# A state-space scan followed by a bilinear feed-forward layer: a new program order, with B and C taken in float32 by head

## The chip, the cores and the metric

The kernel runs on one core of a Trainium2 chip. The core has five engines that work side by side and meet through semaphores: PE multiplies matrices (PEld is its loading of weights), DVE and ACT work on vectors and evacuate PE's results from PSUM, POOL works on vectors in SBUF, and SP issues transfers, which 16 DMA engines carry out. The metric is device time in microseconds from the start to the end of one execution.

## The reference

The inputs are x (4 batches, 8 heads, 768 positions, 32 wide), a (one decay a position), B and C (16 wide), and the matrices w1, w2 (256 x 1024), w3 (1024 x 1024) and w_out (1024 x 256).

```python
for c in range(nc):                               # chunks of positions
    cum = np.cumsum(la, axis=-1)                  # la = log(clip(a))
    M = np.einsum('bhin,bhjn->bhij', Cc, Bc) * np.exp(cum_i - cum_j) * causal
    y = einsum(M, xc) + einsum(Cc, state) * exp(cum)
    state = exp(sum(la)) * state + sum_j(Bc_j * xc_j * exp(cum_last - cum_j))
x = y.transpose(0, 2, 1, 3).reshape(B * S, H * D) # 3072 tokens of 256
out = (((x @ w1) * (x @ w2)) @ w3) @ w_out
```

The matrices arrive as 64-bit floats, so every weight has to be turned into float32 on the chip, out of its two 32-bit words.

## The kernel before

**Slabs and chunks.** The 768 positions are cut into 8 slabs of 96, each slab into two chunks of T = 48 (so 16 chunks, c0 to c15; the chunk length is free, since the state is carried exactly). A slab of all four batches has 384 tokens.

**A chunk** (`chunk`, line 286) makes the decays with two bf16 matmuls (`decay`, 298, tile `pd`) and an exponential on ACT (`expo`, 304, into R); POOL scales B (`bw`, 309); `cb` (314) multiplies C by B into `pc`; DVE weights it with the decays (`weigh`, 328); `Mx` (333) multiplies by x into `py`. XE holds x with two heads in one block-diagonal 128 x 64 operand, so 16 products do a chunk's 32 heads and batches. `Z` (346) transposes the state out of `py` and DVE copies it into the next chunk's XE in four small copies; `hi` and `lo` (361, 365) leave the output as two float32r parts in xT.

**B and C.** For the first slab `cb` uses float32 operands laid out by `load_first`. For the others each is loaded raw, split into three bf16 parts on ACT, DVE and POOL (`split_slab`, 225), written to DRAM, read back packed six times 16 rows high (`load_pack`, 249), and multiplied in bf16 with 96 rows.

**The layer.** `up` (487) makes one column tile of 128 of x @ w1 and of x @ w2 for a slab, each as six float32r products of high and low parts. `gate_a` (506, ACT) evacuates the first, `gate_b` (510, DVE) multiplies by the second, `gate_hi` (513, ACT) and `gate_lo` (518, POOL) make the two parts, and `down` (523) multiplies by w3 @ w_out, which the chip makes once: 16 steps `v*.M` (454) of 4 float32 products each, accumulated in four PSUM banks, then split by `e*.a` and `e*.b`.

**Weights.** `from_f64` (384) does one item of 512 KB: load (D), scaling (A), a byte copy (Y), shift and mask (L), shift and or (S); items of w1 and w2 have two more steps, H and P, for the two parts. There are 8 items `w*`, 4 items `o*` (w_out) and 16 items `v*` (w3). ON_VECTOR (46) and ON_POOL (49) say where some steps run.

**Order.** For the first two slabs PLAN (21) is an order written out by hand: each name is a step, issued in that order on its engine, and "+24" is 24 matmuls of zeros (`keep_clock`, 578). From line 590 on the scheduler is free to order everything but PE, and the loop at line 607 does one slab after another: `up`, then `down`, with the next slab's two chunks between the `up` tiles. All loads and stores are issued by SP. PSUM has four banks for the scan and four for the layer.

Of the kernel before, what the change touches and what calls it, by code (L numbers as in the profile page):

```python
# [45 lines left out]
ON_VECTOR = """
o0.A o1.Y o2.Y o3.A v0.A v0.Y v11.A v14.A v3.Y v5.A v7.Y v8.Y w0.H w1.Y w2.A w3.H w3.Y w4.A w5.H w6.A w6.H
""".split()
ON_POOL = "s1.rB s1.rC s2.rB".split()

@with_exitstack
def kernel(
# [31 lines left out]
    N, D = Bn.shape[2] * 2 // (CPS * NB * H), x.shape[3] // (NB * H)  # L84
    TE = T + N
    HP = H // 2
    TOK = NB * SL
# [6 lines left out]
    NGF = 11  # L94

    const = ctx.enter_context(tc.tile_pool(name="const", bufs=1))
    work = ctx.enter_context(tc.tile_pool(name="work", bufs=2))
    dram = ctx.enter_context(tc.tile_pool(name="dram", bufs=1, space=bass.MemoryType.DRAM))
    ps_at = ctx.enter_context(tc.tile_pool(name="ps_at", bufs=4, space=bass.MemoryType.PSUM))
    ps_l = ctx.enter_context(tc.tile_pool(name="ps_l", bufs=1, space=bass.MemoryType.PSUM))  # L100
# [10 lines left out]
    def load(*args):  # L111
        return ins(nc.sync.dma_start(*args))

    def acopy(*args):
        return ins(nc.scalar.copy(*args))  # L115

    def vtt(*args):
        return ins(nc.vector.tensor_tensor(*args))  # L118

    def vcopy(*args):  # L120
        return ins(nc.vector.tensor_copy(*args))  # L121

    def ptt(*args):
        return ins(nc.gpsimd.tensor_tensor(*args))  # L124
# [3 lines left out]


    GF = const.tile([P, NGF, TOK], F32, name="gf")  # L130
    gf_turn = [0]

    def next_gf():
        gf_turn[0] += 1
        return GF[:, (gf_turn[0] - 1) % NGF]

    G8 = NB * HP // 2
    NK = 2 * CPS * 2
    first = GF.rearrange("p a s -> p (a s)")
    C0 = first[:, :NK * G8 * T].rearrange("p (k g t) -> p k g t", k=NK, g=G8)  # L140
    B0 = first[:, NK * G8 * T:NK * (G8 * T + TE)].rearrange("p (k m) -> p k m", k=NK)
    zero = const.tile([P, 512], BF16, name="zero")
    nc.vector.memset(zero, 0.0)
    BN = [const.tile([P, CPS, NB * HP, N], F32, name=f"bn{i}") for i in range(2)]

    NG = NB * HP
    RI, RJ = T, T + 6
    KD = RJ + 3 * NG  # L150
    LD = const.tile([KD, 2, TE], BF16, name="ld")
    RD = const.tile([KD, NG, T], BF16, name="rd")
# [3 lines left out]
    XE = [const.tile([P, NB * HP, 2 * D], F32, name=f"xe{i}") for i in range(2)]  # L156

    NSLOT = 6
    KS = NSLOT * N
    BP = const.tile([KS, NB * HP, CPS, 2, TE], BF16, name="bp")  # L160
    CP = const.tile([KS, NB * HP, CPS, 2, T], BF16, name="cp")


    Q, SQ = P // (NB * H), a.shape[1]
    arkc = work.tile([P, 3, SQ], F32, name="arkc", tag="g", bufs=FT + 1)
    ar, keep, cum = [arkc[:, i] for i in range(3)]
    ct = GF[:, NGF - 1].bitcast(BF16)[:, :3 * SQ].rearrange("p (t s) -> p t s", t=3)
# [4 lines left out]
    def task(name):  # L172
        def put(f):
            tasks[name] = f
            return f
        return put

    @task("k.p")
    def _():
# [7 lines left out]
        for h2 in range(2):  # L187
# [8 lines left out]

    task("k.C")(lambda: ins(nc.gpsimd.memset(C0, 0.0)))
    task("k.X0")(lambda: ins(nc.gpsimd.memset(XE[0], 0.0)))
    task("k.X1")(lambda: ins(nc.gpsimd.memset(XE[1], 0.0)))
    task("k.L")(lambda: vcopy(LD, ldc))  # L200
    task("k.R")(lambda: vtt(RD, rdc.unsqueeze(1).broadcast_to([KD, NG, T]), rdg.unsqueeze(2).broadcast_to([KD, NG, T]),
                            ALU.add))
    task("a")(lambda: load(ar, a))
    task("a.clip")(lambda: ins(nc.vector.tensor_scalar(ar, ar, 1e-6, 1.0, ALU.max, ALU.min)))
    task("a.ln")(lambda: ins(nc.scalar.activation(ar, ar, AF.Ln)))
    task("a.scan")(lambda: ins(nc.vector.tensor_tensor_scan(cum, keep, ar, 0.0, ALU.mult, ALU.add)))
    task("a.t0")(lambda: vcopy(ct[:, 0], cum))
    task("a.r0")(lambda: vtt(cum, cum, ct[:, 0], ALU.subtract))
    task("a.t1")(lambda: vcopy(ct[:, 1], cum))
    task("a.r1")(lambda: vtt(ct[:, 2], cum, ct[:, 1], ALU.subtract))  # L210
    task("a.save")(lambda: load(cd.rearrange("q h g t s -> (q h g) (t s)"), ct.rearrange("p t s -> p (t s)")))


    NQ = P // N
    XW = [t.shape[2] // NQ for t in (Bt, Ct)]
    dparts = [[dram.tile([3, N, NQ * XW[w]], BF16, name=f"d{'bc'[w]}{k}") for k in range(NSL)] for w in range(2)]

    RUNS = ((0, 3, 0, 0), (3, 2, 0, 1), (5, 1, 0, 2))  # L220

    def load_slab(sl):
        load(BN[sl % 2].rearrange("p c g n -> p (c g n)"), Bn[sl])

    def split_slab(sl, w):
        p, k = f"s{sl}.", "BC"[w]
        v = {}

        def part(t):
            return v["o"][:, (t, 2 - t)[w]]  # L230

        def raw():
            v["r"] = work.tile([P, 512], F32, name="raw")[:, :XW[w]]
            v["o"] = work.tile([P, 3, 512], BF16, name="part")[:, :, :XW[w]]
            load(v["r"], (Bt, Ct)[w][sl].rearrange("n (q x) -> (n q) x", q=NQ))

        def rest():
            (ptt if p + "r" + k in ON_POOL else vtt)(v["r"], v["r"], part(0), ALU.subtract)

        return [  # L240
            (p + "R" + k, raw),
            (p + "a" + k, lambda: acopy(part(0), v["r"])),
            (p + "r" + k, rest),
            (p + "b" + k, lambda: acopy(part(1), v["r"])),
            (p + "c" + k, lambda: ptt(part(2), v["r"], part(1), ALU.subtract)),
            (p + "W" + k, lambda: load(dparts[w][sl].rearrange("t n (q x) -> (n q) t x", q=NQ), v["o"])),
        ]

    def load_pack(sl, w):
        dst, src = (BP, CP)[w], dparts[w][sl]  # L250
        for s, n, *t0 in RUNS:
# [3 lines left out]
    def load_x(c):  # L255
        xe = XE[c % 2]
        for h2 in range(2):
            load(xe[64 * h2 + N:64 * h2 + TE].rearrange("p g d -> p (g d)"), x[c, h2])
# [447 lines left out]
```

## Time and profile before

| what | us |
|---|---|
| median of 3 runs (lowest, highest) | 325.01 (323.97, 327.65) |
| the profiled execution | 325.25 |
| its span, first to last instruction | 323.5 |
| PE, DVE, ACT, POOL busy in it | 297.9, 156.1, 147.9, 117.5 |
| first `up` product | 40.87 |
| first `down` product | 107.13 |
| first product of slab 2 | 141.37 |
| last product | 319.52 |

The profile is one execution. In its page, a row of a group reads: line, engine, operation, output<-inputs, shapes, count | busy, mean ns of one | idle time before them and what ended it. A timeline row reads: start, duration, engine, line, operation, and in brackets the idle time just before and its releaser. Nearly all of PE's instructions carry line 109, that of the helper `mm`, so they are told apart by their tiles. Transfers by kind, in issues and size:

```profile
## 3 DMA queue, kind: packets, MB, share of 16 engines
q1 hardware_dynamic: 26224, 44.89, 54.3%
...
st<-in_w3t_dram SPq DMA_DIRECT2D x16, 512.0 KB
xe<-in_x_dram SPq DMA_DIRECT2D x32, 192.0 KB
st<-in_w_dram SPq DMA_DIRECT2D x8, 512.0 KB
db<-part SPq DMA_DIRECT2D x7, 384.0 KB
bp<-db SPq DMA_DIRECT2D x7, 384.0 KB
```

### The profile page before, as it was taken

To read this page: it belongs to the slowest core of one execution; us is meant where nothing else is said; L and a number is where in the kernel's file an instruction comes from. 1 tells how busy PE (TensorE), PEld (TensorE's weight loads), DVE (VectorE), ACT (ScalarE), POOL (GpSimd) and SP (SyncE) were. 2 spreads that over 40 slices of the span, in tenths; PEclk is the share of its full clock that TensorE was granted. 3 is DMA by queue.
4 is the path that set the end of the run, shared out by engine and by line. 5 is a ranking of instruction groups with operands and counts; after the bars stand their busy time and mean duration, and the time that the engine had idled before them with its cause. 6 is when DMAs were issued, how large, how long until landed. Compare 5 with 4: busy or idle time off the path is not lost. (4 is left out here: it accounts for less than half of the span.)

```text
span 323.5 us, 6505 instructions
## 1 busy us (share of the span) xinstructions
PE 297.9 (92%) x2523; PEld 266.0 (82%) x2523; DVE 156.1 (48%) x288; ACT 147.9 (46%) x279; POOL 117.5 (36%) x142
## 2 busy tenths in 40 slices
PE   8695697887997799899999999999999999999995
PEld 3452587776996599799899999999989999999995
DVE  2879969688871632456331651256035405411210
ACT  4366696677671653343523441453145324422430
POOL 8027358415223272333522341342134304421430
PEclk9899699799999799799999999999999999999999
DMA  7599599997999676844581177129402930001001
GB/s 212 181 307 291 163 272 184 280 243 224 335 207 253 195 138 182 227 140 110 118 156 35 51 151 129 29 54 190 95 21 56 187 79 5 3 16 34 0 4 46
DMA packets 26255, 45.31 MB, mean 140 GB/s; under 512 B 7600, under 2 KB 17200, under 8 KB 25552
## 3 DMA queue, kind: packets, MB, share of 16 engines
q1 hardware_dynamic: 26224, 44.89, 54.3%
q8 instruction: 20, 0.33, 0.4%
q14 instruction: 11, 0.09, 0.1%
HBM read 36.77 MB, written 8.11 MB: 139 GB/s over the span
## 5 line engine op out<-in xcount | busy, mean ns | idle before, releaser
L124 POOL TENSOR_TENSOR g<-gf,g 128x384 fp32r<-128x384 f32 x64 | 66.2, 1037 | 98.0 <-ACT g L115 98.0
L109 PE MATMUL bank<-woh,g 128*128 128x256 f32 x384 | 75.3, 291 | 3.1 <-DVE wol L118 2.2
L118 DVE TENSOR_TENSOR gf<-gf,bank 128x384 f32<-128x384 f32 x48 | 26.5, 552 | 103.6 <-PE bank L109 100.7
L109 PEld LDWEIGHTS bank<-woh,g 128*128 128x128 f32 x384 | 62.4, 196 | 5.1 <-DVE wol L118 2.9
L115 ACT COPY gf<-bank 128x384 f32<-128x384 f32 (+1 forms) x72 | 31.7, 444 | 58.7 <-PE bank L109 50.5
L115 ACT CAST g<-gf 128x384 fp32r<-128x384 f32 x64 | 32.9, 514 | 54.7 <-DVE gf L118 51.7
L109 PE MATMUL bank<-wol,g 128*128 128x256 f32 x192 | 55.2, 287 | 0.0
L109 PE MATMUL bank<-xT,w1h 128*128 128x384 f32 x192 | 52.8, 355 | 0.1
L109 PE MATMUL bank<-xT,w2h 128*128 128x384 f32 x192 | 48.8, 335 | 0.0
L109 PEld LDWEIGHTS bank<-wol,g 128*128 128x128 f32 x192 | 37.6, 196 | 0.0
L109 PE MATMUL bank<-wof,mag 128*128 128x256 f32 x128 | 33.0, 410 | 2.6 <-DVE wof L420 2.6
L109 PEld LDWEIGHTS bank<-xT,w1h 128*128 128x128 f32 x192 | 33.1, 188 | 2.1 <-DVE xT L118 0.4
L109 PEld LDWEIGHTS bank<-xT,w2h 128*128 128x128 f32 x192 | 34.8, 188 | 0.0
L109 PE MATMUL bank<-xT,w1l 128*128 128x384 f32 x96 | 32.2, 335 | 0.0
L109 PE MATMUL bank<-xT,w2l 128*128 128x384 f32 x96 | 32.2, 335 | 0.0
L109 PEld LDWEIGHTS bank<-wof,mag 128*128 128x128 f32 x128 | 25.9, 206 | 7.3 <-DVE wof L420 3.0
L115 ACT COPY st<-st 128x512 uint8<-128x512 uint8 x20 | 27.4, 1370 | 7.6 <-DVE mag L402 7.4
L124 POOL TENSOR_TENSOR R<-bn,R 128x128 f32<-128x128 f32 x32 | 14.7, 478 | 43.3 <-issue 36.5
L124 POOL TENSOR_TENSOR part<-raw,part 128x512 bf16<-128x512 f32 (+1 forms) x14 | 15.9, 1137 | 33.3 <-ACT part L115 33.3
L121 DVE COPY xe<-Z 16x256 f32<-16x256 f32 x60 | 26.8, 447 | 1.1
L109 PEld LDWEIGHTS py<-R,xe 128*64 128x64 f32 x512 | 17.8, 146 | 11.4 <-DVE R L118 4.4
L115 ACT CAST part<-raw 128x512 bf16<-128x512 f32 (+1 forms) x28 | 16.0, 578 | 24.3 <-DMA raw<-in_Bt_dram 10.9
(69 smaller groups left out, 388.7 us busy)
## 6 DMA issues: line engine op xcount, KB each, us to landing
st<-in_w3t_dram SPq DMA_DIRECT2D x16, 512.0 KB
xe<-in_x_dram SPq DMA_DIRECT2D x32, 192.0 KB
st<-in_w_dram SPq DMA_DIRECT2D x8, 512.0 KB
db<-part SPq DMA_DIRECT2D x7, 384.0 KB
bp<-db SPq DMA_DIRECT2D x7, 384.0 KB
st<-in_w_out_dram SPq DMA_DIRECT2D x4, 512.0 KB
bn<-in_Bn_dram SPq DMA_DIRECT2D x8, 256.0 KB
dc<-part SPq DMA_DIRECT2D x7, 288.0 KB
```

What stands on the lines that cost most here:

```text
L109: return tc.keep_in_program_order(nc.tensor.matmul(*args, **kw))
L115: return ins(nc.scalar.copy(*args))
L118: return ins(nc.vector.tensor_tensor(*args))
L121: return ins(nc.vector.tensor_copy(*args))
L124: return ins(nc.gpsimd.tensor_tensor(*args))
```

## The change

The whole program is now one written order; every step names its engine where there is a choice ("w0.Y:v" is DVE, ":a" ACT, ":p" POOL), and nothing is left to the scheduler. The order of slabs is three `up`s, two `down`s, and then one of each in turn, written "uuu01u2u3u4u5u67", so the gated products of three slabs are kept (GF has 24 places instead of 11, XT three instead of two) and their high and low parts are made only shortly before their `down`. An item `w*` now holds one column tile of both w1 and w2 (rows of 1 KB instead of 4 KB), so that `up` of tile k needs item k alone; these come first. An item `v*` holds two row blocks and two column blocks of w3, and the 16 steps now fill one PSUM bank four times, a pair of column tiles after the other. While three `up`s run, `up` has three PSUM banks (four afterwards); the scan keeps four.

B and C are loaded by head in float32 straight from the inputs (3.7 MB in all); the split, the DRAM parts and the packed reads are gone. x is loaded without the zero half of the block diagonal. The sums of log a are saved and read by ACT's queue for the first two chunks. LD and RD are doubled. The fillers are 61 instead of 39.

```diff
+ORDER = "uuu01u2u3u4u5u67"
 PLAN = """
+k.z a.D k.p s0.T s0.N a.clip k.X w0.D k.L0 a.ln a.exp a.scan c0.X a.t0 a.r0 c1.X a.t1 a.r1 k.R0 w1.D a.save:a
++20 c0.C w2.D k.L1 k.R1 s1.T w0.A:a c0.K:a w3.D w0.Y:v s1.N w0.L c1.K:a w0.S w0.H:v w4.D w1.A:a w0.P:v w1.Y:a
++25 c0.D0 c0.D1 c2.K w2.A:v c0.E0 w1.L c0.E1 w1.S c0.B0 w2.Y:a c0.B1 +6 c1.D0 c0.M0 w5.D c0.M1 +2 c1.D1 c3.K
...
+c1.Z w2.P:p c3.X w3.L w3.S c4.K c1.h c1.x0:a c1.l w7.D c1.x1:a c1.x2:v l0.0.0 c1.x3:a w3.H:v w5.A:a w3.P:v
...
+l6.7.l:p l7.0.h l7.3.0:4 l7.2.g l7.0.l:p l7.3.1:4 l7.3.a l7.4.0:4 l7.3.g l7.4.1:4 l7.4.a l7.5.0:4 l7.4.g
+l7.5.1:4 l7.5.a l7.6.0:4 l7.5.g l7.6.1:4 l7.6.a l7.7.0:4 l7.6.g l7.7.1:4 l7.7.a z6.0 l7.7.g z6.1 y6.0 y6.0d z6.2
+y6.1 y6.1d l7.1.h l7.2.h l7.1.l:p l7.3.h l7.2.l:v l7.4.h l7.3.l:p l7.5.h l7.4.l:v l7.6.h l7.5.l:p l7.7.h
+l7.6.l:v y6.2 l7.7.l:p y6.2d z7.0 z7.1 y7.0 y7.0d z7.2 y7.1 y7.1d y7.2 y7.2d
...
+            pl_bank[k] = bank[4 + ring % (4 if DOWNS or len(UPS) >= NLAG else 3)]
...
+    def load_bc(sl, e=None):
+        for hf, (rest, one) in enumerate(((Bt, b0), (Ct, c0))):
+            for h2 in range(2):
+                r = 32 * (2 * hf + h2)
+                load(BC[r:r + N, sl % 2].rearrange("p g c m -> p (g c m)"), rest[sl - 1, h2] if sl else one[h2], eng=e)
...
+        @step("C")
+            for g in range(G8):
+                for hf in range(2):
+                    for h2 in range(2):
+                        r = 32 * (2 * hf + h2)
+                        b = BC[r:r + N, sl % 2, g, cc]
+                        mm(v["pc", hf][64 * h2:64 * h2 + 64, g], b[:, 0:TE], b[:, TE:], start=True, stop=True)
...
+        @step("Y")
+            for kt in range(KT):
+                for b in range(NB):
+                    for q in range(4):
+                        g, rows = b * HP + 2 * kt + q // 2, slice(64 * (q % 2), 64 * (q % 2) + 64)
+                        mm(v["py"][32 * q:32 * q + 32, kt, b, :], xe[rows, g], R[rows, g, :], start=True, stop=True)
...
+    def w12_item(ft):
+        def loads(st):
+            for i, w in enumerate((w1, w2)):
+                yield (st[:, i * GR:(i + 1) * GR].rearrange("p (k c) -> p k c", k=KT),
+                       w.rearrange("(k p) c -> p k c", p=P)[:, :, 2 * ft * P:2 * (ft + 1) * P])
...
+        fp, k0 = j // 4, j % 4 * 2
+        src = w3t.rearrange("(k p) c -> p k c", p=P)[:, k0:k0 + 2, 4 * fp * P:4 * (fp + 1) * P]
```

The step names: `a.*` log a and its sums, `c*.D/E/B/C/M/Y/Z/x/h/l` the parts of a chunk in the order of the text above (`cb` is now C, `Mx` is Y), `c*.K` and `c*.X` the loads of the sums and of x, `s*.T` and `s*.N` those of B and C, `l*.*.0/1/a/g/h/l` the two halves of `up` and the four gate steps, `z` a third of `down`, `y` its evacuation and `y..d` its store.

More of the change, by code (lines that the diff above doesn't have):

```diff
@@ L137, with load @@
[L137 to L141, printed above, removed]
-    zero = const.tile([P, 512], BF16, name="zero")
-    nc.vector.memset(zero, 0.0)
-    BN = [const.tile([P, CPS, NB * HP, N], F32, name=f"bn{i}") for i in range(2)]
-    NG = NB * HP
+    def load(*args, eng=None):
+        return ins({None: nc.sync, "a": nc.scalar}[eng].dma_start(*args))
@@ new lines, in copy, with tt @@
+    def copy(eng, *args):
+        return ins(nc.scalar.copy(*args) if eng == "a" else {"v": nc.vector, "p": nc.gpsimd}[eng].tensor_copy(*args))
+    def tt(eng, *args):
+        return ins({"v": nc.vector, "p": nc.gpsimd}[eng].tensor_tensor(*args))
+    W12 = const.tile([P, FT, 2, 2, KT, P], F32R, name="w12")
+    WO = [const.tile([P, FT, DM], F32R, name=f"wo{p}") for p in "hl"]
+    wof = const.tile([P, FT, DM], F32, name="wof")
+    GF = const.tile([P, NGF, TOK], F32, name="gf")
+    XT = const.tile([P, 3, 2, KT, NB, SL], F32R, name="xt")
@@ new lines @@
+    XE = const.tile([P, 2, NG, D], F32, name="xe")
+    RR = const.tile([P, 2, NG, TE], F32, name="rr")
+    BN = const.tile([P, 2, CPS, NG, N], F32, name="bn")
+    BC = const.tile([P, 2, G8, CPS, TE + T], F32, name="bc")
+    ZZ = const.tile([P, KT, NB, D], F32, name="zz")
+    OB = const.tile([P, 3, DM], F32, name="ob")
+    spare = const.tile([P, 1], F32, name="spare")
+    zero = const.tile([P, 512], BF16, name="zero")
+    bank = [ps.tile([P, 512], F32, name=f"bank{i}") for i in range(8)]
@@ new lines, with st_of, mag_of, g_of @@
+    ST = pool.tile([P, NST, 2 * GR], F32, name="st")
+    MAG = pool.tile([P, NMAG, GR], F32, name="mag")
+    G = []
+    def st_of(i):
+        return ST[:, i % NST]
+    def mag_of(i):
+        return MAG[:, i % NMAG]
+    def g_of(sl, ft):
+        if not G:
+            passing.close()
+            pool = ctx.enter_context(tc.tile_pool(name="parts", bufs=1))
+            G.append(pool.tile([P, NG2, 2, TOK], F32R, name="g"))
+        return G[0][:, (DOWNS.index(sl) * FT + ft) % NG2]
+    def gf_of(sl, ft):
+        return GF[:, (UPS.index(sl) * FT + ft) % NGF]
@@ L214 @@
[L214 to L247, printed above, removed]
@@ L286, in chunk, with step @@
     def chunk(c):
         sl, cc = divmod(c, CPS)
-        xe = XE[c % 2]
-        bn = BN[sl % 2][:, cc]
-        ld = LD.rearrange("p h m -> p (h m)")
-        half = NB * HP // 2
+        xe, R, bn = XE[:, c % 2], RR[:, c % 2], BN[:, sl % 2, cc]
+        ld = LD[:, c % 2].rearrange("p h m -> p (h m)")
+        hi, lo = [XT[:, sl % 3, i] for i in range(2)]
         v = {}
-        steps = []
-        def step(name, *args):
-            return lambda f: steps.append((f"c{c}." + name, lambda: f(*args)))
+        def step(name):
+            return task(f"c{c}." + name)
@@ L372, in chunk @@
-        return [first, second, steps[:1], steps[1:]]
-    for c in range(2 * CPS):
-        task(f"c{c}.X")(lambda c=c: load_x(c))
-        task(f"c{c}.K")(lambda c=c: load_cum(c))
-        for stage in chunk(c):
-            tasks.update(stage)
-    W12 = [[const.tile([P, KT, DF], F32R, name=f"w{i}{p}") for p in "hl"] for i in (1, 2)]
-    WO = [const.tile([P, FT, DM], F32R, name=f"wo{p}") for p in "hl"]
-    def from_f64(name, src, dst=None):
+                    for q in range(4):
+                        g, rows = b * HP + 2 * kt + q // 2, slice(64 * (q % 2), 64 * (q % 2) + 64)
+                        mm(v["py"][32 * q:32 * q + 32, kt, b, :], xe[rows, g], R[rows, g, :], start=True, stop=True)
@@ new lines, in chunk, with _, carry @@
+        if c + 1 < NCH:
+            @step("Z")
+            def _(e):
+                ins(nc.vector.transpose(ZZ.rearrange("p k b d -> p (k b) d"),
+                                        v["py"].rearrange("p k b m -> p (k b) m")[:, :, 0:32]))
+            def carry(q, e):
+                xn = XE[:, (c + 1) % 2].rearrange("p (b k g) d -> p g b k d", b=NB, g=2)
+                h2 = q % 2
+                copy(e, xn[64 * h2:64 * h2 + N, q // 2], ZZ[32 * q:32 * q + N].rearrange("p k b d -> p b k d"))
+            for q in range(4):
+                step(f"x{q}")(lambda e, q=q: carry(q, e))
@@ L390, in from_f64, with _ @@
+        sv = slice(cc * T, (cc + 1) * T)
+        step("h")(lambda e: copy("a", hi[:, :, :, sv], v["py"][:, :, :, N:]))
+        step("l")(lambda e: tt("v", lo[:, :, :, sv], v["py"][:, :, :, N:], hi.bitcast(F32)[:, :, :, sv], ALU.subtract))
+    for c in range(NCH):
+        chunk(c)
+    order_of = [0]
+    def from_f64(name, loads, dst=None):
         v = {}
+        turn = order_of[0]
+        order_of[0] += 1
         @task(name + ".D")
-        def _():
-            v["st"] = work.tile([P, 2 * GR], F32, name="st", bufs=4)
-            load(v["st"].bitcast(U32).rearrange("p (f k) -> p f k", f=src.shape[1]), src)
+        def _(e):
+            v["st"] = st_of(turn)
@@ L436 @@
-    wof = const.tile([P, FT, DM], F32, name="wof")
+    def w12_item(ft):
[3 more added lines that the diff above has]
+                       w.rearrange("(k p) c -> p k c", p=P)[:, :, 2 * ft * P:2 * (ft + 1) * P])
+        v = from_f64(f"w{ft}", loads)
+        hi, lo = [W12[:, ft, l].rearrange("p i k c -> p (i k c)") for l in range(2)]
+        task(f"w{ft}.H")(lambda e: copy(e, hi, v["mag"]))
+        task(f"w{ft}.P")(lambda e: tt(e, lo, v["mag"], hi.bitcast(F32), ALU.subtract))
@@ L438, in wo_item @@
     def wo_item(j):
         n = GR // DM
[L440 to L447 removed]
+        from_f64(f"o{j}", lambda st: [(st.rearrange("p (f k) -> p f k", f=n),
+                                       w_out[n * j * P:n * (j + 1) * P, :].rearrange("(f p) k -> p f k", p=P))],
+                 wof[:, n * j:n * (j + 1)].rearrange("p f k -> p (f k)"))
@@ L467, with _ @@
-    for j in range(2 * DF // GR * KT):
-        w12_item(j)
+        def _(e):
+            if k0 == 0:
+                mm(acc3, zero[:, 0:P], zero, start=True, stop=False)
+            for k in range(2):
+                for f in range(2):
+                    mm(acc3[:, f * DM:(f + 1) * DM], v["mag"].rearrange("p (k f c) -> p k f c", k=2, f=2)[:, k, f],
+                       wof[:, k0 + k], start=False, stop=(k0 + k == FT - 1 and f == 1))
+    for ft in range(FT):
+        w12_item(ft)
     for j in range(FT * DM // GR):
@@ L578, in keep_clock @@
     def keep_clock(n):
         for _ in range(n):
-            alone = len(bank) - 1 not in opened
-            mm(bank[-1], zero[:, 0:P], zero, start=alone, stop=alone)
+            mm(bank[6], zero[:, 0:P], zero, start=True, stop=True)
     for name in PLAN.split():
```

524 lines of the change are left out of this document (202 added, 322 removed).

## The prediction

> **What bounds the kernel now.** I read the page's busy shares and slices first, then windows over three stages, then the PE timeline.
>
> ```profile
> span 323.5 us, 6505 instructions
> PE 297.9 (92%) x2523; PEld 266.0 (82%) x2523; DVE 156.1 (48%) x288; ACT 147.9 (46%) x279; POOL 117.5 (36%) x142
> ...
> PEclk9899699799999799799999999999999999999999
> DMA  7599599997999676844581177129402930001001
> ```
>
> PE is busy 92% of the span; no other engine reaches half. The granted clock dips only in the first half, where DMA is also dense.
>
> ```profile
> 0.00:41.00 41.00, 30.95 (x164) 17.33 (x164) 31.71 (x55) 22.48 (x31) 19.07 (x33) 0.88 0.76 233
> 41.00:141.40 100.40, 88.97 (x695) 80.17 (x693) 63.75 (x111) 59.44 (x103) 42.32 (x41) 0.95 0.84 222
> 141.40:324.00 182.60, 177.95 (x1670) 168.50 (x1668) 60.67 (x124) 65.94 (x145) 56.11 (x68) 1.00 0.34 74
> 172.25:202.87 30.62, 30.51 (x302) 28.67 (x301) 11.63 (x24) 11.44 (x25) 9.59 (x12) 1.00 0.47 94
> 294.40:311.05 16.65, 16.65 (x99) 16.65 (x98) 3.88 (x7) 7.26 (x16) 6.65 (x7) 1.00 0.03 9
> 311.05:319.85 8.80, 8.75 (x73) 8.55 (x71) 0.55 (x1) 1.26 (x3) 1.43 (x2) 1.00 0.13 32
> ```
>
> Columns: stretch, length, busy time (and instructions) of PE, its weight loads, DVE, ACT and POOL, granted clock, DMA share, GB/s. The last two rows price one slab: 16.65 us for the products with w1, w2 (`up`) and 8.80 for the product with the last matrix (`down`). The fourth row is one whole period in mid-kernel: 30.62, so two chunks cost 30.62 - 16.65 - 8.80 = 5.17, 2.6 each, and PE stands still for 0.1 of it. From 141 us on there is little to win: PE does its own list. What can be won lies before that: the first 41 us contain five w3 steps and the first chunks; in the next 100 PE is idle 11.4 and runs at 0.95 of its clock, some 16 us together.
>
> **The small matmuls, which the change rebuilds.**
>
> ```profile
> 21.34 1.51 PE L109 MATMUL pc<-gf 128*64 128x384 f32 x8
> ...
> 86.49 3.62 PE L109 MATMUL bank<-wof,mag 128*128 128x256 f32 x16
> 89.76 0.70 PE L109 MATMUL pl<-xT,w1h 128*128 128x384 f32 x2
> ...
> 92.02 3.62 PE L109 MATMUL bank<-wof,mag 128*128 128x256 f32 x16
> ...
> 146.42 0.69 PE L109 MATMUL pc<-cp,bp 96*64 96x48 bf16 x32
> 147.04 0.62 PE L109 MATMUL bank<-xT,w1h 128*128 128x384 f32 x2
> ...
> 149.33 1.15 PE L109 MATMUL py<-R,xe 128*64 128x64 f32 x32
> 150.41 0.62 PE L109 MATMUL bank<-xT,w1h 128*128 128x384 f32 x2
> ```
>
> A full-width float32 product runs as two instructions. From 86.49 to 92.02 are 5.53 us for 16 of 256 columns and one column tile of `up` (16.65 / 8 = 2.08): 3.45 / 16 = 0.216 us each, so 1.72 per w3 step and 0.84 ns a column. At that price 64 columns take 0.054 and the 32 `py` instructions 1.73 one after another; they take 1.08 (149.33 to 150.41). The eight of 384 columns at 21.34 would take 2.6 and take 1.51. So two outputs in different column halves of the array run side by side. Nothing here uses different row groups.
>
> **The change, part by part.**
>
> *C and B in float32.* Now `cb` is 32 bf16 instructions a chunk (0.62 us to the next start); then it is 32 products of 48 columns, 64 instructions on four tiles (16 rows by 64 columns each). Its weights have 64 columns, so I take 0.054 each, not the 0.040 of 48 columns. All four at once: 64 x 0.054 / 4 = 0.87; two at once, as the rows show for column halves: 1.73; one at once: 3.5; the lowest end is 64 x 0.040 / 4 = 0.65. [...]
>
> [...]
>
> *`Mx` becomes `Y`.* 32 instructions over 128 rows and a 64-column half become 64 over 64 rows and a 32-column quarter, in four different quarters. Four at once: 64 x 0.054 / 4 = 0.87, two at once for the old ones 32 x 0.054 / 2 = 0.87: no change. Two at once: +0.87; one: +2.6. The decay products stay. A chunk thus costs 2.6 + 0.35 = 2.95 on PE.
>
> *What goes away, and what moves between engines.* Splitting B and C into bf16 parts, their way out to DRAM and back, and the zero half of x.
>
> ```profile
> L124 POOL TENSOR_TENSOR part<-raw,part 128x512 bf16<-128x512 f32 (+1 forms) x14 | 15.9, 1137 | 33.3 <-ACT part L115 33.3
> ...
> L115 ACT CAST part<-raw 128x512 bf16<-128x512 f32 (+1 forms) x28 | 16.0, 578 | 24.3 <-DMA raw<-in_Bt_dram 10.9
> ```
>
> ```profile
> SPq L112 <- POOL part L124: 27.7, 10, 8.5
> ```
>
> ACT loses 16.0 us of casts, POOL 15.9, SP 27.7 of waiting. ACT takes over four more byte copies (1.37 each, below), six more scalings (0.69) and 36 of the 60 carry copies (at 0.37, a small ACT copy's time at 319.88 below): 5.5 + 4.1 + 13.3 = 22.9, so its sum grows by 7. POOL gives 20 of its 64 low parts to DVE (20 x 0.55 = 11), which loses the carries. All of this lies beside PE: in the second half PE waits 0.1 a period, so I credit it with nothing there. If the cover went, those 7 us of ACT would be its price.
>
> *The start.*
>
> ```profile
> 1.25 8.62 PE L109 MATMUL bank<-zero 128*128 128x512 bf16 x26 [1.25 <-DVE zero L143]
> ...
> 20.91 0.49 PE L109 MATMUL pd<-rd,ld 102*128 102x384 bf16 x2
> ...
> 22.78 2.12 PE L109 MATMUL bank<-zero 128*128 128x512 bf16 x9
> ...
> 34.99 1.98 PE L109 MATMUL py<-R,xe 128*64 128x64 f32 x32 [4.00 <-DVE R L118]
> ...
> 40.87 0.79 PE L109 MATMUL pl<-xT,w1h 128*128 128x384 f32 x2
> ```
>
> ```profile
> 5.82 0.26 DVE L204 TENSOR_SCALAR arkc<-arkc 128x192 f32<-128x192 f32 x1 [4.62 <-DMA arkc<-in_a_dram]
> ...
> 12.29 0.35 DVE L118 TENSOR_TENSOR gf<-arkc,gf 128x192 bf16<-128x192 f32 x1
> ```
>
> ```profile
> L118 DVE TENSOR_TENSOR R<-pc,R 128x384 f32<-128x384 f32 x32 | 16.6, 548 | 0.3 <-PE pc L109 0.3
> ...
> L307 ACT ACTIVATE R<-pd 128x384 f32<-128x384 f32 x32 | 15.0, 505 | 6.4 <-PE pd L109 6.4
> ```
>
> ```profile
> 12.67 0.34 SPq L112 DMA_DIRECT2D cd<-gf  x1
> ...
> 14.57 0.36 SPq L112 DMA_DIRECT2D ld<-cd  x1
> ```
>
> Now the sums of log a are ready at 12.6 because weight pieces stand between the steps on DVE, and the second chunk's `py` waits 4.0 for DVE. `up` begins at 40.87. After it, `a` is the first load and the seven steps stand together (about 2.4 of DVE and ACT instead of 6.8): ready at 8, saved and read again (12.67 to 14.57, 1.9) at 10, landed by 13 to 14. The reads and the save move from SP to ACT's queue: seven issues of some 0.35, 2.5 us of ACT, which w1's conversion waits behind. PE first does 20 fillers (8.62 x 20/26 = 6.6), `C` (1.2) and 25 fillers (0.236 each by the nine: 5.9): the first decay at 15. Then two exponentials 1.0 (505 ns each), two weightings 1.1 (548), `Y` 1.2, transpose and copies 1.7 (an estimate: five small operations on two engines), the next chunk's weightings with a weight piece 1.5, `Y` 1.2, then the conversion pieces that ACT and DVE hold ahead of the last parts, 2.5: `up` at 26. Lower end 24 (nothing held), upper 33 (loads as late as now).
>
> *Three `up` passes before the first `down`.* The order moves the eight conversions of w1, w2 ahead and lets w3 and w_out come within the next two passes.
>
> ```profile
> L115 ACT COPY st<-st 128x512 uint8<-128x512 uint8 x20 | 27.4, 1370 | 7.6 <-DVE mag L402 7.4
> L115 ACT COPY gf<-bank 128x384 f32<-128x384 f32 x48 | 23.0, 479 | 15.6 <-PE bank L109 12.5 <-POOL g L124 3.1
> L420 DVE SCALAR_TENSOR_TENSOR mag<-mag,st 128x512 uint32<-128x512 uint32 x24 | 21.4, 892 | 0.3
> L118 DVE TENSOR_TENSOR gf<-gf,bank 128x384 f32<-128x384 f32 x48 | 26.5, 552 | 103.6 <-PE bank L109 100.7 <-PE pd L109 1.5 <-ACT gf L115 1.4
> L414 DVE TENSOR_SCALAR st<-st 128x512 int32<-128x512 int32 x28 | 16.2, 578 | 7.7 <-ACT st L115 7.4
> L404 ACT ACTIVATE mag<-st 128x512 f32<-128x512 f32 x19 | 13.1, 687 | 10.7 <-DMA st<-in_w_dram 5.3 <-DMA st<-in_w3t_dram 5.3
> ```
>
> In the first pass the plan gives ACT seven scalings, seven byte copies, seven evacuations and eight small pieces: 4.8 + 9.6 + 3.4 + 3.8 = 21.6; PE 16.65 + 2 x 2.95 = 22.5. In the second ACT has 32.6 and PE 16.65 + 8 x 1.72 + 5.9 = 36.3. So PE stays the longest list, but ACT at 90 to 96% holds evacuations behind byte copies while only three PSUM banks serve `up`. I charge 4 us in each of these passes, 2 in the third, 2 for the rest (the last two `down`s follow each other with no `up` between, and the second needs seven casts and subtractions after the first): 12, against some 16 us in the present second stage. Ends 2 and 24 (that stage's loss half again).
>
> **The sum**, in one profiled execution:
>
> ```profile
> 319.88 0.37 ACT L115 COPY gf<-bank 128x256 f32<-128x256 f32 x1 [2.50 <-PE bank L109]
> 320.28 0.79 SPq L112 DMA_DIRECT2D out_dram<-gf  x2
> ```
>
> Start 26; eight slabs 8 x 25.45 = 203.6; w3 16 x 1.72 = 27.5; chunks 2 to 15, 14 x 2.95 = 41.3; losses 12; the tail as now, 323.5 - 319.8 = 3.7. Together 314.1 of span. The profiled execution took 325.25 for its span of 323.5, so 1.75 more: 315.9, against 325.25, and the median of the runs, 325.01, is 0.2 lower. I predict 316.
>
> **Rivals.**
>
> *Row groups do not overlap.* Two tiles at a time in `C` and `Y`: 2 x 0.87 x 14 = 24 us, 340; if only one of the two suffers, 328. It decides from 9 / 14 = 0.65 us a chunk on. For it: no row shows row groups side by side. Against it: `py` runs two tiles freely, and the four of `Y` write four different column quarters. [...]
>
> *ACT becomes the bound.* The byte copies and evacuations of the first two passes hold PE as the present second stage does, or the start slips to 33: 7 to 12 more, 325. For it: ACT's 21.6 against 22.5. Against: DVE and POOL lose the splitting, DMA (0.84 in that stage) loses its round trip.
>
> *No loss at all.* Losses 2 and a start at 25: 305.
>
> *The order changes nothing.* The start is only shifted: five w3 steps (8.6 us) come out of it and return later; with a start at 33 this is the second rival's time.
>
> **How the numbers follow.** Forecast (tiles overlap, PE first) 0.55, its own range 309 to 322; no loss 0.10; ACT the bound 0.15; one small product at half rate 0.07; both 0.13. Range 303 to 332: it holds all but the last case and the fringe, some 0.17. A measurement of this kernel tells about 1% (3.25) from no change: below 321.8 lie nearly all of the first two, 0.64; within 1% part of ACT's case and the edges, 0.15; above 328.3 the rest, 0.21.
>
> **What would show it.** `pc` at about 0.9 and `py` at about 0.9 us a chunk (1.7 each would be the first rival); the first `up` at 24 to 28; a mid-kernel period near 31.4; PE idle in the first two passes below 8 us, and what ends it ACT's `gf`; SP no longer waiting for POOL's `part`. A period above 33, or a first `up` after 33, makes the forecast wrong.

## The result and the profile after

The changed kernel takes 312.24 us (median of 4 runs, 307.66 to 313.07), the kernel before 325.31 in the runs beside it: a ratio of 0.954, 95% interval 0.942 to 0.967. A second set of runs of the same kernel gave 313.66 us (311.99 to 314.96), ratio 0.962 (0.956 to 0.968). The profiled execution took 313.07 us, its span is 311.0; it is the longest of the four and counts as slow, so that the ratio is of the mean of the other three, 310.7, to that of the kernel before, 325.6. The head of its page and slices:

```profile
span 311.0 us, 8592 instructions
...
PE 295.3 (95%) x3613; PEld 266.9 (86%) x3617; DVE 139.3 (45%) x262; ACT 152.1 (49%) x293; POOL 70.0 (23%) x99
...
DMA  7984837976776000611116111601010100010011
...
q1 hardware_dynamic: 20996, 27.11, 33.6%
```

The main queue's transfers fell from 44.89 to 27.11 MB, and DMA has little to do from the fourteenth slice on. ACT grew by 4 us, POOL lost 47. The windows view, with the columns as before: the start, roughly the three `up` passes (a pass has eight column tiles of 12 products; the first stretch has nine of them), one whole period in mid-kernel, and its `down`.

```profile
0.00:32.50 32.50, 22.68 (x321) 11.48 (x324) 16.90 (x34) 15.10 (x23) 7.78 (x27) 0.89 0.78 193
32.50:61.40 28.90, 27.74 (x431) 25.20 (x433) 22.57 (x45) 22.27 (x35) 4.06 (x4) 0.94 0.72 195
61.40:97.50 36.10, 35.42 (x355) 31.57 (x355) 25.94 (x51) 28.68 (x44) 2.29 (x4) 1.00 0.75 228
97.50:132.10 34.60, 34.55 (x411) 30.98 (x411) 16.70 (x32) 17.34 (x34) 8.23 (x10) 1.00 0.20 41
180.06:210.99 30.93, 30.93 (x430) 29.19 (x429) 10.87 (x22) 12.67 (x29) 7.77 (x10) 1.00 0.26 52
171.55:180.06 8.51, 8.51 (x73) 8.51 (x73) 0.56 (x1) 1.21 (x4) 0.00 (x0) 1.00 0.16 42
```

PE stands still 1.2 us in the first pass, 0.7 in the second and 0.1 in the third. The period is 30.93; with `up` at 16.65 and `down` at 8.51, two chunks take 5.77, 2.88 each. What ended PE's idle time between the first `up` and about 141 us, in the waits view (total, times, longest): first the longest three of the kernel before, 41 to 141 us, then the changed one, 32.5 to 141. The 1.6 for `xt` ended at 32.54, ahead of the first `up`, and belongs to the start.

```profile
PE bank L109 <- DVE wol L118: 2.2, 2, 1.3
PE pc L109 <- DMA cp<-dc: 1.9, 1, 1.9
PE pl L109 <- DVE gf L118: 1.7, 2, 1.4
...
```

```profile
PE bank L148 <- ACT xt L154: 1.6, 1, 1.6
PE bank L148 <- DVE xt L157: 0.9, 1, 0.9
PE bank L148 <- DVE wol L157: 0.7, 1, 0.7
PE bank L148 <- ACT gf L154: 0.2, 1, 0.2
```

Ten different releasers became four. (The helper's line is 148 here, and two lower in most experiments, where the written order fills fewer lines.) The sum, term by term, in the profiled span:

| term | predicted | after |
|---|---|---|
| first `up` product at | 26 | 32.5 |
| eight `up` and `down` | 203.6 | 8 x (16.65 + 8.51) = 201.3 |
| 16 steps of w3, at 1.72 as before | 27.5 | 27.5 |
| 14 chunks | 41.3 | 14 x 2.88 = 40.3 |
| tail | 3.7 | 3.7 |
| losses, the remainder | 12 | 5.7 |
| span | 314.1 | 311.0 |

The same count for the kernel before, from its first `up` on: 323.5 - 40.87 = 282.6, less 203.6, 11 w3 steps 18.9, 14 chunks at 2.6 = 36.4 and the tail 3.7, leaves 20.0 of losses. Ahead of its first `up` it did five w3 steps (8.6) and two chunks (5.2): 27.1 of other time there, against 32.5 - 5.8 = 26.7 now. So in this execution the start won 0.4, and the 12.5 us of span are in the main 14.3 of losses after it and 2.3 of `down`, less about 4 for dearer chunks. `up` is taken as before here (the last pass takes 16.68); why `down` takes 8.51 instead of 8.80 no row shows.

A second profiled execution of the same kernel, from the second set, has a span of 309.9, and its first `up` stands at 30.21. Behind it come a slow `C` and 24 slow products of `up`, which take 1.15 and 4.44 us in mid-kernel; later sections return to them:

```profile
34.40 1.96 PE L148 MATMUL bank<-bc 16*64 16x48 f32 x64
36.29 5.92 PE L148 MATMUL bank<-xt,w 128*128 128x384 f32 x24
```

By the same count its start has 24.4 of other time, 2.7 less than the kernel before, and its losses are 6.9. Over the seven profiles that share this start (this one, the one above and five of the experiments below) the first `up` stands at 30.2 to 32.5. So the start is worth 0.4 to 2.7 us, and differences of 2 us in it mean nothing.

### The profile page after: what moved, and what is told of

The parts are those of the page before. It is cut to its first block, busy times and chain, and to the rows that moved or that the text cites. A ratio compares the mean times of both kernels' runs of the same rounds, so it can differ in the third digit from the quotient of the medians.

```text
span 311.0 us, 8592 instructions
## 1 busy us (share of the span) xinstructions
PE 295.3 (95%) x3613; PEld 266.9 (86%) x3617; DVE 139.3 (45%) x262; ACT 152.1 (49%) x293; POOL 70.0 (23%) x99
## 3 DMA queue, kind: packets, MB, share of 16 engines
q1 hardware_dynamic: 20996, 27.11, 33.6%
## 4 chain that ended last, share of the span: by engine, by line
PE 79%; DMA 11%; ACT 3%; DVE 2%; POOL 1%; issue 1%; POOLq 0%; ACTq 0%; SPq 0%; DVEq 0%
PE bank L148 79%; DMA st<-in_w3t_dram 5%; DMA rd<-cd 2%; DMA cd<-gf 1%; ACT st L154 1%; DMA ld<-cd 1%; POOL g L157 1%; ACT mag L412 1%; DMA bc<-in_Bt_dram 1%; DMA gf<-in_a_dram 1%; DVE st L425 1%; DVE mag L431 0%; POOLq L624 0%; DVE gf L157 0%; ACT xe L154 0%
## 5 line engine op out<-in xcount | busy, mean ns | idle before, releaser
L148 PE MATMUL bank<-xt,w 128*128 128x384 f32 x768 | 146.6, 343 | 2.6 <-ACT xt L154 1.6
L148 PEld LDWEIGHTS bank<-xt,w 128*128 128x128 f32 x768 | 133.1, 189 | 5.9 <-ACT xt L154 1.8
L157 POOL TENSOR_TENSOR g<-gf,g 128x384 fp32r<-128x384 f32 x44 | 48.0, 1113 | 122.8 <-PE bank L148 77.1
L154 ACT COPY gf<-bank 128x384 f32<-128x384 f32 x64 | 31.2, 489 | 40.0 <-PE bank L148 39.6
L157 POOL TENSOR_TENSOR rr<-bn,rr 128x128 f32<-128x128 f32 x32 | 14.9, 483 | 92.1 <-ACT rr L330 79.3
L148 PEld LDWEIGHTS bank<-wof,mag 128*128 128x128 f32 x128 | 24.1, 190 | 3.9 <-issue 0.8
L412 ACT ACTIVATE mag<-st 128x512 f32<-128x512 f32 x25 | 17.0, 684 | 15.4 <-DMA st<-in_w3t_dram 6.1
L157 DVE TENSOR_TENSOR g<-gf,g 128x384 fp32r<-128x384 f32 x20 | 18.4, 936 | 12.7 <-ACT g L154 12.7
L157 DVE TENSOR_TENSOR rr<-bank,rr 128x384 f32<-128x384 f32 x32 | 16.3, 550 | 13.3 <-PE bank L148 11.9
L148 PEld LDWEIGHTS bank<-bc 16*64 16x64 f32 x1024 | 17.0, 138 | 5.6 <-issue 5.6
L148 PEld LDWEIGHTS bank<-rr,xe 64*32 64x32 f32 x1024 | 15.5, 109 | 4.9 <-issue 4.3
```

Of the source, the lines that this page charges most:

```text
L148: return tc.keep_in_program_order(nc.tensor.matmul(*args, **kw))
L154: return ins(nc.scalar.copy(*args) if eng == "a" else {"v": nc.vector, "p": nc.gpsimd}[eng].tensor_copy(*args))
L157: return ins({"v": nc.vector, "p": nc.gpsimd}[eng].tensor_tensor(*args))
L412: ins(nc.scalar.activation(v["mag"], v["wh"], AF.Copy, scale=2.0 ** -112))
```

## The experiments

Each is a variation of the changed kernel, if nothing else is said; times are medians, ratios are to the kernel before in the same runs. The second set of runs above is the first entry:

> The changed kernel unaltered, as the yardstick beside the next three. Every theory expects 312 (307 to 314).

### Four tiles at once, or two

```diff
-            for g in range(G8):
-                for hf in range(2):
+            for hf in range(2):
+                for g in range(G8):
                     for h2 in range(2):
...
-            for kt in range(KT):
+            for pp in range(2):
+              for kt in range(KT):
                 for b in range(NB):
-                    for q in range(4):
+                    for q in range(2 * pp, 2 * pp + 2):
```

> The products of C and of Y in another order, so that only two different tiles of the array stand near each other in the program. Theory (tiles run side by side, but only those that are near each other in the program; PE's list is the bound): C and Y take 1.7 to 1.9 us to the next start instead of 1.08 and 1.03, a mid-kernel period 34 instead of 30.9, the time 312 + 14 x 1.6 = 334. Rival 1 (the tiles' work is held in queues of their own, and the order in the program does not matter): C, Y and the time unchanged, 312. Rival 2 (PE has room beside its list): C and Y longer, the time below 320.

329.97 us, ratio 1.016 (1.008 to 1.024): 16.3 more than the changed kernel in the same runs. PE's timeline of the changed kernel, then of this one:

```profile
157.15 1.10 PE L148 MATMUL bank<-rr,xe 64*32 64x64 f32 x64
158.18 4.44 PE L148 MATMUL bank<-xt,w 128*128 128x384 f32 x24
...
162.88 1.15 PE L148 MATMUL bank<-bc 16*64 16x48 f32 x64
163.96 4.44 PE L148 MATMUL bank<-xt,w 128*128 128x384 f32 x24
```

```profile
162.78 1.79 PE L148 MATMUL bank<-rr,xe 64*32 64x64 f32 x64
164.50 0.79 PE L148 MATMUL bank<-xt,w 128*128 128x384 f32 x3
...
169.21 1.88 PE L148 MATMUL bank<-bc 16*64 16x48 f32 x64
```

To the next start, `Y` takes 1.03 in the changed kernel and 1.72 here, `C` 1.08 and 1.81 (169.21 to 171.02, where 24 of `up` begin). The 1.72 is 64 x 0.054 / 2 = 1.73, two at a time; 1.03 and 1.08 are 3.4 and 3.2 at a time. (The 0.054 is worked out from full-width products; no run has one tile at a time.) The 64 instructions are the same; only their order differs. The four tiles of `C` share two column halves, so that more than two at a time means row groups that overlap. They do here, where products for different tiles stand next to each other in the order (1.08 us), and not where only two tiles stand together (1.81). In `C` the new order also changes whether neighbours write one PSUM bank or two; `Y` writes one bank in both orders, so there the order alone made the difference.

PE's own list sets the time here. From the first `down` on, the two profiles differ by 11.5 us over eight chunks, 1.4 each and all of it; a period takes 33.82 instead of 30.93. Over the six chunks between the first `up` and the first `down` they differ by 5.8 instead of 8.6; there the changed kernel had the lower clock, 0.89 for 0.94 in the first pass, and the slow `C` and `up` of the second profile, shown above.

### One part at a time

The kernel before, with B and C loaded by head in float32 and the splitting and its way through DRAM taken out; order, weights and x as before:

```diff
-            task(f"s{sl}.P{'BC'[w]}")(lambda sl=sl, w=w: load_pack(sl, w))
-            tasks.update(split_slab(sl, w))
+            task(f"s{sl}.R{'BC'[w]}")(lambda sl=sl, w=w: load_bc(sl, w))
...
-                    mm(pcv[64 * h2:64 * h2 + 64, g], BP[:, hf * half + g, cc, h2], CP[:, hf * half + g, cc, h2],
+                    mm(pcv[64 * h2:64 * h2 + 64, g], w[:, 0:TE], w[:, TE:], start=True, stop=True)
```

> The kernel before with one part of the change alone: B and C by head in float32 from slab 1 on, no split, no way through DRAM; order, weights, x and engines as before. Theory (the order with the weights first brings the gain, float32 B and C cost PE 0.3 us a chunk in the loop and 1.3 a chunk in the written part, where two tiles stand alone, and give little back): 320 to 332. Rival (what ACT, DVE, POOL and the transfers are relieved of is the gain): 310 to 317.

325.14 us, ratio 0.999 (0.996 to 1.002): no gain, alone. The second stage:

```profile
41.00:141.40 100.40, 92.85 (x896) 84.90 (x896) 53.95 (x100) 49.48 (x82) 28.97 (x31) 0.97 0.51 131
```

DMA's share in the second stage falls from 0.84 to 0.51, and PE comes further: slab 2 begins at 135.42 instead of 141.37, its first `up` having come at 37.92 instead of 40.87. It does so although `C`, whose two halves stand apart in the old order, costs 1.06 for each (102.40 to 103.46), 2.1 a chunk instead of 0.62. From there on a period takes 31.53 instead of 30.62, 4.6 us over five periods, and most of the 6 us are given back. So the zero is a balance: the relief is worth something before 141 us, and the dear `C` of the old order takes it away behind.

The third `up` before the first `down` taken out again; PLAN rearranged by that alone:

```diff
-ORDER = "uuu01u2u3u4u5u67"
+ORDER = "uu0u1u2u3u4u5u67"
```

> The changed kernel with the first down after two up passes instead of three: the last eight w3 steps and the casts of the first slab's products stand without the third up pass between them, which follows the first down. Theory (the third pass covers the end of the weights and the casts; without it PE waits there 5 to 9 us, above all around the four evacuations of the single bank): 317 to 322. Rival (the weights are ready in time anyway): 311 to 314.

321.77 us (317.11 to 323.51), ratio 0.982 (0.970 to 0.993): against the 312 to 314 of the changed kernel the third pass is worth 6 to 9 us, no closer, since the runs of this kernel scatter. The profiled execution was the shortest (span 315.0) and shows what takes its place, PE's waits:

```profile
PE bank L146 <- DVE wol L155: 2.8, 2, 1.4
PE bank L146 <- DVE mag L429: 2.4, 1, 2.4
```

The first `down` now needs the last split of the combined matrix, and a weight's last step just when they are made.

### The bytes that were taken away

Copies from DRAM to DRAM put back 2.46 MB a slab for seven slabs, together 17.2 of the 17.8 MB that fell away, in six issues on SP each:

```diff
+    junk = dram.tile([6, 50, w3t.shape[1]], U32, name="junk")
+    def copy_rows(sl):
+        for n in range(6):
+            load(junk[n], w3t[100 * n + 50:100 * n + 100, :])
```

> The changed kernel with transfers put back: for each slab from the second on 2.46 MB are copied inside DRAM (rows of w3, read by nobody) in six issues of SP, 17.2 MB in all, as much as the split of B and C moved before, three slabs' worth of it before the first down. Theory (the second stage gained by its order, not by relief of the DMA engines): 312 to 316. Rival (the relief of DMA is the gain): 319 to 326, with PE waiting for st or for sums.

322.21 us, ratio 0.992 (0.988 to 0.995): most of the gain is gone, as the rival expected. But a copy inside DRAM both reads and writes there: the page counts 61.7 MB read and written, the kernel before 44.9. What the burden was worth in the kernel before is therefore known only roughly. Two more kernels keep three of the copies, all ahead of the first `down`, or the other four, behind the last w3 step:

> The changed kernel with three of the seven 2.46 MB copies, those that stand between the first product of slab 0 and the first down step, while the weights are still loaded. The output is the same. With all seven the time was 322.2 us, 8.5 more than the changed kernel in the same runs. Theory: bytes cost time only where they make the weights late, so these three cost nearly all of it: 319 to 323 us. Rival: every byte moved costs the same wherever it is moved (three sevenths of 8.5 us): 316 to 318 us.

> The changed kernel with the other four of the seven 2.46 MB copies, all behind the products of w3 and w_out, where no weight is loaded any more. The output is the same. Theory: they are hidden, 311.5 to 314.5 us. Rival, every byte costs the same (four sevenths of 8.5 us): 317 to 319 us.

Early: 322.57 us, ratio 0.991 (0.987 to 0.994). Late: 311.83 us, ratio 0.957 (0.952 to 0.962). Four copies where no weight is loaded cost nothing, three while weights load cost all that seven do. How, in the timelines of the early one: SP, then ACT, then PE.

```profile
60.79 4.51 SPq L149 DMA_DIRECT2D junk<-in_w3t_dram x6
65.41 2.76 SPq L149 DMA_DIRECT2D st<-in_w3t_dram x4
```

```profile
74.11 0.66 ACT L418 ACTIVATE mag<-st 128x512 f32<-128x512 f32 x1 [9.95 <-DMA st<-in_w3t_dram]
74.81 1.35 ACT L152 COPY st<-st 128x512 uint8<-128x512 uint8 x1
75.88 0.60 ACT L152 COPY gf<-bank 128x384 f32<-128x384 f32 x1
```

```profile
76.53 2.29 PE L146 MATMUL bank<-xt,w 128*128 128x384 f32 x6 [6.97 <-ACT gf L152]
```

This is a chain worth learning to read. The weights of one item are late: their load is issued behind the copies, which cost SP 4.5 us, and lands at 74.03, 8.62 us after its issue, where loads of w3 on the changed kernel's chain take 4.8 to 7.0; the 16 DMA engines are busy 0.96 of that time. How much of the delay is SP's issuing and how much the bytes ahead was not told apart. ACT stands 9.95 us before that item's scaling; the evacuation of a finished `up` bank (`gf`) is two instructions behind it and starts only at 75.88; so PE, which needs that bank, stands 6.97 us. PE's row names ACT; the cause is a transfer. And PE then runs slower for a while: the eight instructions of a w3 step take 3.53 us here and 1.89 in the changed kernel; the granted clock is 0.60 from 74 to 84 us. The copies differ from the old traffic in row length, in what they do to DRAM and in SP's issue time, so this shows the mechanism, and only roughly its size in the kernel before.

### The start

The sums of log a saved and read by SP ahead of the weights, instead of by ACT behind them:

```diff
-k.z a.D k.p s0.T s0.N a.clip k.X w0.D k.L0 a.ln a.exp a.scan c0.X a.t0 a.r0 c1.X a.t1 a.r1 k.R0 w1.D a.save:a
-+20 c0.C w2.D k.L1 k.R1 s1.T w0.A:a c0.K:a w3.D w0.Y:v s1.N w0.L c1.K:a w0.S w0.H:v w4.D w1.A:a w0.P:v w1.Y:a
+k.z a.D k.p s0.T s0.N a.clip k.X k.L0 a.ln a.exp a.scan a.t0 a.r0 a.t1 a.r1 k.R0 a.save w0.D c0.X +20 c0.C k.L1 k.R1
+c0.K w1.D c1.K c1.X w2.D s1.T w0.A:a w3.D w0.Y:v s1.N w0.L w0.S w0.H:v w4.D w0.P:v +10 c0.D0 c0.D1 c2.K c0.E0 c0.E1
```

> The changed kernel with the sums of log a saved and read by SP ahead of the weights (w0 and x behind the save, w1 and the rest behind the first read), and 10 fillers instead of 25 before the first decay. Theory (the save, 4.5 us, and the reads, 4 to 5 us, stand behind the weights' bytes in the DMA engines): first decay at 11 to 12 us instead of 15.5, first up at 27 to 30 instead of 32.5, the time 307 to 310. Rival (the conversion on ACT and DVE sets the start): first up still at 31 to 34, the time 311 to 314.

317.45 us, ratio 0.974 (0.969 to 0.979), above both expectations: the first chunk came early (`Y` at 15.77), but now the third chunk's sums were read behind the weights, and PE's order has a product of them ahead of chunk 1's work:

```profile
25.69 0.50 PE L146 MATMUL bank<-rd,ld 102*128 102x384 bf16 x1 [8.82 <-DMA ld<-cd]
```

The time is not that of the sums alone. This order also loads the sixth weight item over the second before the second's last two steps (so one column tile of w1 and w2 is not computed from its own weights, with the same amount of work), and DVE stands 7.95 us for that load, with chunk 0's transpose behind it. The filler products are 46 instead of 61.

The next kernel moves that decay product behind chunk 1, and the loads of the fourth and later weight items back, and has 40 fillers; the one after it has the order of the changed kernel and none of the 61 filler products; the last combines both and moves the fourth item's ACT steps out of the way.

> The changed kernel with the sums saved and read by SP ahead of most weights, as in the last run, but with the third chunk's sums read ahead of w3 and its decay after the second chunk's output, so that PE does not stand before it, and with the sixth weight item loaded only after the second is used (in the last run it overwrote it, so the second column tile of w1 and w2 was another's there). Theory (small transfers behind the weights' bytes set the start): first decay near 12, first up at 25 to 28, the time 305 to 309. Rival (the conversion on ACT and DVE sets what PE can do before 60 us): first up earlier, but PE idle in the first pass by as much, 311 to 314.

> The changed kernel without the 61 matmuls of zeros. Theory (they cover waits, and stand on the path only where PE would wait anyway, but hold the clock): the half clock lasts some 10 us longer, first up within 1 us of 32.5, the time 312 to 316. Rival (they are on the path of the start): first up at 28 to 30, 307 to 310.

> The order with the running sums ahead of the weights (310.1 us), without its filler products on PE, and with the fourth weight item's two ScalarE steps moved behind chunk 1's conversion of its output, for which TensorE waited 2.9 us. The output is the same. Theory: the first up step stands at 22 to 25 us instead of 26 and of 32.5 in the changed kernel, the third item's words are not later for it, and the fillers are worth nothing: 306 to 309 us. Rival: the weights' bytes set the pace of the first passes, so what is won ahead of the first up is lost again inside the first pass: 310 to 312 us.

310.1 us (ratio 0.953, 0.947 to 0.960), 310.78 (0.956, 0.951 to 0.962) and 310.21 (0.955, 0.952 to 0.958): by their intervals none differs clearly from the changed kernel. The first `up` stands at 26.1, 30.7 and 24.1 instead of 30.2 to 32.5, so it is earlier in the first and the last alone; yet only 1.5 to 3.5 us come out at the end. The first missed its range, 305 to 309, the second lies between its two, and the last has the rival's time. The first changes the order of the sums and the number of fillers together. The last one's PE timeline shows where part of an earlier start goes:

```profile
24.07 0.69 PE L146 MATMUL bank<-xt,w 128*128 128x384 f32 x1
...
29.22 0.50 PE L146 MATMUL bank<-rd,ld 102*128 102x384 bf16 x1 [2.26 <-DMA ld<-cd]
...
31.57 1.96 PE L146 MATMUL bank<-bc 16*64 16x48 f32 x64
33.46 6.24 PE L146 MATMUL bank<-xt,w 128*128 128x384 f32 x24
```

From the first `up` to the start of the next `Y`, at 39.63, are 15.56 us; the same products take 10.41 in the first profile of the changed kernel (32.54 to 42.95) and 11.94 in the second (30.21 to 42.15). Against the second, the first `up` is 6.1 us earlier, `Y` and the end of the span (307.4 for 309.9) only 2.5. So 3.6 are lost within these few products, and 2.26 of them are the wait for the fourth chunk's sums, whose load took 6.63 us to land. The slow products (1.96 for `C`, 6.24 for 24 of `up`, which take 1.15 and 4.44 elsewhere) cost 2.6 here, but the second profile has them too (1.96 and 5.92), so they explain hardly any of the difference. The rival that named the weights' bytes had the time right; whether bytes take the rest was not shown.

## Why the prediction came out as it did

The time, 312.24 for 316, lies in the forecast's own range; two terms were off by some 4 to 6 us each, in opposite directions. That the sum came this near is luck; that the tiles overlap, on which the forecast rested, is not. Of the signs named, `C`, `Y`, the period (30.93 for 31.4) and the idle time below 8 us came; the first `up` at 24 to 28 did not, and what ends the idle time is not ACT's `gf`.

*Tiles.* The step that carried most doubt held: a chunk costs 2.88, predicted 2.95, and the rival of row groups one after another is excluded by the pair of timelines above. `C` itself takes 1.08 to the next start where 0.97 was taken: 64 x 0.054 / 1.08 is 3.2 tiles at a time, not four. No run shows the 0.1 that the 0.97 holds beside the 0.87 of four tiles at once; the runs show the 1.08 of the whole step and the 2.88 of a chunk. The four tiles of `Y`, two of them in each row half, write one PSUM bank, and take 1.03 where two at a time take 1.72.

*The start, 26 predicted, 30.2 to 32.5 measured.* (The pieces of the prediction add up to 25.2.) What failed is the chain behind the first decay. ACT's queue and PE's timeline of the changed kernel:

```profile
5.84 0.34 ACTq L151 DMA_DIRECT2D cd<-gf  x1
...
10.34 0.39 ACTq L151 DMA_DIRECT2D ld<-cd  x1
...
14.13 0.59 ACTq L151 DMA_DIRECT2D rd<-cd  x2
14.82 0.66 ACT L412 ACTIVATE mag<-st 128x512 f32<-128x512 f32 x1 [4.93 <-DMA rd<-cd]
```

```profile
15.46 0.48 PE L148 MATMUL bank<-rd,ld 102*128 102x384 bf16 x2 [1.83 <-DMA rd<-cd]
...
19.83 0.32 PE L148 MATMUL bank<-rd,ld 102*128 102x384 bf16 x1 [2.58 <-DMA rd<-cd]
...
20.68 1.69 PE L148 MATMUL bank<-rr,xe 64*32 64x64 f32 x64
...
29.62 1.10 PE L148 MATMUL bank<-rr,xe 64*32 64x64 f32 x64
...
32.54 0.44 PE L148 MATMUL bank<-xt,w 128*128 128x384 f32 x1 [1.55 <-ACT xt L154]
```

The sums were saved at 5.84, earlier than the 8 predicted. The save took 4.5 us to land, not 1.9, behind weights that had been issued first, and the two together bring the first decay at 15.46 for 15. So far the sum holds. Then come two things that it does not count. The second chunk's reads, issued only at 14.13, land 5.2 us later, and their product stands ahead of chunk 0's output in PE's order: PE waits 2.58, and chunk 0's `Y` starts at 20.68 where the sum has 17.1. Next, the third chunk's decay (at 24.25, after a wait of 1.88), six fillers and `C` of chunk 1 (at 27.22) stand ahead of chunk 1's output, whose `Y` starts at 29.62 where the sum has 21.5. From there to the first `up` are 2.9 us, for 3.7 predicted. The reads had been priced as issues on ACT and not as waits: ACT too stood 4.93 us before its next scaling and held w1's conversion with it. In the fourth experiment, where the save goes ahead of the weights, the read of it is issued 2.5 us after it.

*The losses, 12 predicted, 5.7 and 6.9 measured.* Four us were charged for each of the first two passes, since ACT's list came to 90 to 96% of PE's. It was 22.3 of 28.9 and 28.7 of 36.1 us, 77 and 79%, and PE waited for an evacuation 0.2 us in all: the mechanism that the term was for hardly occurred. Of the 5.7, 2.0 are PE's idle time in the three stretches, and the granted clock of the first, 0.94 over 28.9 us, is some 1.7, an estimate; the rest was not traced. So the rival in which ACT becomes the bound had the place right and not the condition: here it came with late weights alone. The early copies produced it (9.95 us on ACT, 6.97 on PE), at 322.57 us, near the 325 named for it, though by a transfer and not by ACT's own list. DVE's low parts took 0.94 us each where 0.55 was taken, and PE waited for none of them.

*What carries the gain.* The prediction gave it to the order and credited the missing transfers with nothing of their own but in that rival. The runs show that the relief counts. The new order with the bytes put back keeps 3 us, both together win 13; float32 B and C in the old order come out at 0, but as a balance, since their `C` is dearer there. The four late copies were hidden (311.83 us), the three early ones not (322.57). Which parts of the new order carry the gain beyond the third `up` pass (6 to 9 us), the weight items, the division between engines or the written order, no run separates.

*The order changes nothing*, the last rival, is half true: the start was little more than shifted, 0.4 to 2.7 us of other time; what changed is the stage after it.

## What to carry to other kernels

Ask of every engine that evacuates PE's results what stands ahead of the evacuation in its order, and whether that can wait for a transfer: here a late load reached PE through it, under the evacuation's name (9.95 us on ACT, 6.97 on PE). Judge transfers by when they move: here three copies cost 9 to 10 us while weights were loading, four nothing afterwards. For small products, try those for different tiles of the array next to each other in the order (here 1.03 for 1.72 us a `Y`, 1.08 for 1.81 a `C`), and price an earlier start only by what the first products behind it will then cost (here a first `up` 6.1 us earlier moved the next `Y` by 2.5). Before you price a start, compare two executions of one kernel: here its first `up` moved by 2.3 us between them.

## What was not expected of the hardware

*Half speed that the granted clock does not show.* Without fillers, these are `C` of chunks 0 (58 of its 64 instructions), 1 and 2, and `up` ahead of the last, on PE:

```profile
6.97 1.94 PE L146 MATMUL bank<-bc 16*64 16x48 f32 x58 [0.19 <-DMA bc<-in_c_dram]
...
24.45 1.96 PE L146 MATMUL bank<-bc 16*64 16x48 f32 x64
...
31.66 3.42 PE L146 MATMUL bank<-xt,w 128*128 128x384 f32 x11 [0.31 <-DVE xt L155]
35.01 1.15 PE L146 MATMUL bank<-bc 16*64 16x48 f32 x64
```

The clock row of that page reads 9 in all 40 slices, while the same step takes 1.96 and then 1.15. The first profile of the changed kernel shows a factor of two: its first fillers start 0.43 us apart up to 3.8 us, and 0.22 from 4.3 on, while the windows view gives a granted clock of 1.00 for both. In the rows above `C` is fast 3.35 us after unbroken work began at 31.66. In the last kernel of the section on the start, the unbroken work begins at 29.2 and the slow part lasts, by an estimate from the 1.8 us that 24 of `up` take longer and that factor of two, to about 37, 7.8 us. The fillers are fast some 2.7 us after the first of them in the changed kernel and some 5.8 in the kernel before. No one length fits these four, and no run shows what ends the slow stretch. With fillers half speed is not excluded: the second profile of the changed kernel has 1.96 for `C` and 5.92 for 24 of `up`, and there the granted clock does dip, to 0.89 in that pass. In the first profile it is 0.50 from 34.7 to 38.1 us, where products of `up` start 0.32 us apart instead of 0.17.

*Fillers.* With them `C` of chunk 0 is fast (1.15 us at 6.98), but the granted clock falls to 0.89 in the start and 0.94 in the first pass (0.94 and 0.88 in the second profile), and chunk 1's `C` takes 1.40. Without them the time is 310.78, no worse. What the fillers gain at the start and lose by the clock behind it could not be told apart here.

*A small transfer behind large ones.* Behind weights, the 144 KB of sums landed 4.5 us after their issue, and the reads of 9 and 4.5 KB took 3.7 and 5.2. Ahead of the weights the read that needs the sums was issued 2.5 us after them.
